# Hash-bucket attention and a maxout feed-forward on one core: query and key sets kept in load order, a second pair hashed by heads, the first batch dealt anew

## The chip, the core and the metric

The kernel runs on one core of one Trainium2 chip. The metric is the device time of one execution in microseconds (us); the kernel before took 266.97 us (median of three runs, 266.57 to 268.87). The core's engines are TensorE (PE; its weight loads are listed as PEld), VectorE (DVE), ScalarE (ACT), GpSimd (POOL) and SyncE (SP). ACT, POOL and SP also issue transfers. Each engine works through its own list of instructions in order; the lists are tied together by semaphores only.

## The reference

The inputs q, k and v have 4 batches, 8 heads, 768 tokens and 64 numbers per token and head, all fp32. Cut to what matters:

```
bits(x)  = (x @ proj) > 0                      # proj is 64 x 6: six bits per token and head
mask     = bucket(bits(q)) == bucket(bits(k))  # only tokens with the same six bits see each other
scores   = where(mask, q @ k.T / 8, -1e9)
attn     = softmax(scores) @ v
x        = attn, heads side by side: 3072 tokens x 512
h        = max(x @ w1, x @ w2, x @ w3)         # 512 -> 768
out      = h @ w_out                           # 768 -> 512
```

## The kernel before

**Scores.** For a head, a tile S holds the transposed queries or keys (64 rows, bf16) and below them the bits as +0.5 or -0.5, so that one matmul gives the scaled product plus a term that falls where bits differ. The work is cut into 192 units. A unit is two blocks of 128 keys against 384 queries (half the tokens) of one head: `scores(u)` (L274) issues two matmuls (L283) and ACT takes the exponential of both at once (L285) into one of 26 AT tiles. A batch is 48 units; a half batch of queries is 24, and its feed-forward can start when all eight heads of that half are done. The loop over units (L571) issues, for unit u: scores one or two units ahead, what `when(u, ...)` put down for u, one group of the feed-forward, the additions of AT tiles (`gather`, L327), and at the ends of stretches a `burst` (L542), which multiplies AT with the values (L310), sums AT over the keys (L360), inverts the sums and scales (L379) into the feed-forward's input xT. What is put down for a unit fixes only the place in each engine's list. SP's and POOL's transfers are issued as soon as their list has come to them and their buffer is free.

**First batch.** Its heads come in pairs 0 to 3, loaded in the order (p c): partition p holds tokens 6p to 6p+5. `load_pair` (L121) loads, `pair_group` (L145) transposes on PE (L132) and copies to a T32 tile on DVE or ACT (L138), `pair_place` (L140) scales on POOL into S (L143). Pair 0 is hashed head by head: `first_hash` (L171) puts each head's six rows of bits at the partitions where S wants them, and `first_bits` (L177) writes them from PSUM into S on DVE (L179). Pairs 1 to 3 go through `pair_hash` (L149): four matmuls (L154), one DVE comparison of 128 rows (L158) into a `bits` tile, and four transfers on SP from there into S (L163).

**Later batches.** Queries and keys come in sets of four heads, (side, g), side 1 the keys. `load_quad` (L184) loads a set in four transfers in the order (t cc m): partition t of a head's 32 holds, for each of four cc, six tokens m. `turn` (L193) transposes 32 x 32 blocks on DVE (L198), and writes them with a stride of four numbers, so that the columns stand in the order (m t cc), which is that of the values (`load_v`, L240, again p c). `narrow` (L200) scales to bf16 on POOL (L203), `place` (L207) moves to S by SP (L209), `quad_hash` (L212) hashes. Sets 2 and 3 belong to batch 1 and are dealt by hand inside the first batch; later ones follow a formula.

**Feed-forward.** `ffn_groups` (L385) gives, for half h (0 to 7), 18 groups of four matmuls (L394), six blocks of 128 hidden numbers by three weights, and six groups of the second product (L422). Of each block the first of three is copied from PSUM to ht as fp16 (L398, on ACT for even blocks and DVE for odd ones, on ACT at the end), and the next two are taken into ht as maxima by DVE (L400). The output rows of a block are set by `block_of`. From unit 39 one group is issued per unit.

**PSUM.** Score tiles rotate over s0 to s2 and all others over m0 to m3; s2 lies on m2 and m3 and is opened when unit MORE is issued (`lay_out`, L78).

Of the kernel before, what the change touches and what calls it, by code (L numbers as in the profile page):

```python
# [17 lines left out]
def kernel(  # L18
# [12 lines left out]
    nc = tc.nc  # L31
# [139 lines left out]
    def first_hash(bp, side, hd):  # L171
        for par in range(2):
            j = 2 * side + par
            nc.tensor.matmul(bp[Q * j : Q * j + NBITS, 0:HALF], pj2[:, par : 2 * NBITS : 2],
                             t32[0][:, side, hd * HALF : (hd + 1) * HALF], start=True, stop=True)

    def first_bits(bp, side, hd, par):  # L177
        j = 2 * side + par
        nc.vector.tensor_scalar(out=s_of[0][D : D + NBITS, 2 * side + hd, par * HALF : (par + 1) * HALF],  # L179
                                in0=bp[Q * j : Q * j + NBITS, 0:HALF], scalar1=0.0, scalar2=0.5,  # L180
                                op0=AluOp.is_gt, op1=AluOp.subtract)
# [11 lines left out]
    def turn(name, u, half):  # L193
        if name not in t32:
            t32[name] = t32_pool.tile([P, 2, S], FP32, tag="T32", name="T32")
        i_ = nat[name].rearrange("p (cc m u d) -> p u m cc d", cc=CC, u=2, d=Q)[:, u, half * MH : (half + 1) * MH]
        o = t32[name][:, u, half * HALF : (half + 1) * HALF].rearrange("p (m t cc) -> p m cc t", t=Q, cc=CC)
        nc.vector.transpose(o, i_)  # L198
# [40 lines left out]

    def load_v(g):  # L240
        b, h0 = divmod(4 * g, H)
        nc.gpsimd.dma_start(v_tile(g)[:], v[b, h0 : h0 + 4].rearrange("h (p c) d -> p h (c d)", p=P))
# [84 lines left out]
    def gather(u):  # L327
        g, hd, kp = unit_of(u)
        if u < 48 or kp == 0:
            return  # L330
        if kp == 1:
            as_of[g, hd] = as_pool.tile([P, 2, HALF], FP16, tag="as", name="As")
        t, new = as_of[g, hd], at_tiles[u % NAT][:, :, 0:HALF]
        old = at_tiles[(u - 1) % NAT][:, :, 0:HALF] if kp == 1 else t[:]
        nc.vector.tensor_tensor(out=t[:], in0=old, in1=new, op=AluOp.add)  # L335
        if kp == 2 and u >= 144:
            nc.vector.tensor_tensor(out=t[:, 0, :], in0=t[:, 0, :], in1=t[:, 1, :], op=AluOp.add)
# [47 lines left out]
    def ffn_groups(h):  # L385
        b, qh = divmod(h, 2)
        xt = xts.pop(h)
        hts, gs = {}, []
        for fb in range(NFB):
            for wi in range(3):  # L390
                def go(fb=fb, wi=wi):
                    ps = ps_tile("l1")
                    for jc in range(NJC):
                        nc.tensor.matmul(ps[:, 0:HALF], w_sb[wi][:, jc, fb * P : (fb + 1) * P], xt[:, jc, :],  # L394
                                         start=(jc == 0), stop=(jc == NJC - 1))
                    if wi == 0:
                        hts[fb] = h_pool.tile([P, HALF], FP16, tag="ht", name="ht")
                        (nc.vector.tensor_copy if fb % 2 and not ended else nc.scalar.copy)(hts[fb][:], ps[:, 0:HALF])  # L398
                    else:
                        nc.vector.tensor_tensor(out=hts[fb][:], in0=hts[fb][:], in1=ps[:, 0:HALF], op=AluOp.max)  # L400
                gs.append(go)
# [35 lines left out]
    with tc.manual_schedule():  # L437
# [9 lines left out]
        load_pair(3, nc.sync)  # L447
        load_quad(1, 2, range(4), nc.sync)
# [12 lines left out]
        load_v(0)  # L461
# [8 lines left out]
        pair_keep(0, 0, 0, mq, nc.scalar.copy)  # L470
# [40 lines left out]
        for u, side, g, eng in ((8, 0, 2, nc.sync), (25, 1, 3, nc.sync), (27, 0, 3, nc.sync)):  # L511
            when(u, load_quad, side, g, range(4), eng)
        hash_at = {}
        for g in range(2, NPAIR // 2):
# [16 lines left out]
            hash_at[{2: 33, 3: 48}.get(g, UPB * b2 - 24 + 24 * i2)] = g  # L531
# [3 lines left out]
        ffn_at = {39: 0, 57: 1, **{24 * (h + 1) + 9: h for h in range(2, 2 * B - 1)}}  # L535
# [101 lines left out]
```

## Time and profile before

| | |
|---|---|
| median of three runs | 266.97 us |
| profiled execution, its own time | 268.83 us |
| its span, first to last instruction | 267.0 us |
| mean granted TensorE clock | 0.987 |
| exponentials on ACT | 192, 153.0 us |
| weights, values, queries and keys read from HBM | 25.17 MB |

A profile page gives busy time of each engine; the span in 40 slices; the chain of work that ended last; and groups of instructions by line, engine, operation and tile, with the mean time of one and the idle time before them. The windows view gives busy time in chosen stretches and the granted clock. The timeline lists instructions in order of time. A wait is put down to what came last by the profile.

### The profile page before, as it was taken

How to read it: one execution, taken by the hardware profiler on the slowest of the kernel's cores; microseconds unless marked ns; L12 is line 12 of the kernel's file. 1: busy time of each engine (PE TensorE's matmuls, PEld its weight loads, DVE VectorE, ACT ScalarE, POOL GpSimd, SP SyncE). 2: the span in 40 equal slices, each digit the busy share in tenths (PEclk: the TensorE clock that was granted, in tenths of full speed). 3: DMA queues.
4: the chain of work that ended last, by engine and by line, in shares of the span. 5: the costliest groups of instructions: out<-in, count | busy, mean ns of one | idle time of the engine just before them, and what ended most of it. 6: DMA issues, size and time to landing. Idle time of an engine off the chain costs nothing. (4 is left out here: it accounts for less than half of the span.)

```text
span 267.0 us, 5948 instructions
## 1 busy us (share of the span) xinstructions
PE 256.7 (96%) x2247; PEld 141.0 (53%) x2247; DVE 207.9 (78%) x447; ACT 177.8 (67%) x256; POOL 63.8 (24%) x104
## 2 busy tenths in 40 slices
PE   7969979999999999999999999999999999999995
PEld 3535424555555554555555554555555555564552
DVE  2823897887989899889989899889848995886361
ACT  4977956683898179953898189954898289802322
POOL 3693642560151413440151312110000000000000
PEclk9997988999999999999999999999999999999999
DMA  6989999988055731973064821920030002000303
GB/s 210 341 170 234 158 273 205 218 167 200 6 153 144 178 77 39 189 216 105 1 159 139 185 68 39 196 61 18 0 119 2 2 0 87 33 1 2 118 0 118
DMA packets 21171, 30.96 MB, mean 116 GB/s; under 512 B 2696, under 2 KB 15896, under 8 KB 21144
## 3 DMA queue, kind: packets, MB, share of 16 engines
q0 software_dynamic: 7936, 12.59, 24.8%
q1 hardware_dynamic: 12920, 17.62, 20.7%
q8 instruction: 17, 0.28, 0.4%
q10 hardware_dynamic: 288, 0.39, 0.4%
q14 instruction: 10, 0.08, 0.1%
HBM read 25.17 MB, written 6.29 MB: 118 GB/s over the span
## 5 line engine op out<-in xcount | busy, mean ns | idle before, releaser
L285 ACT ACTIVATE AT<-sc 128x768 f16<-128x768 f32 x192 | 153.0, 817 | 58.1 <-PE sc L283 53.2
L394 PE MATMUL l<-xT,w_sb 128*128 128x384 f16 x568 | 112.3, 326 | 0.1
L283 PE MATMUL sc<-S 72*128 72x384 bf16 (+1 forms) x384 | 92.9, 330 | 5.1 <-POOL T L203 2.0
L394 PEld LDWEIGHTS <-w_sb 128*128 128x128 f16 x576 | 55.4, 97 | 39.4 <-DVE xT L379 1.2
L400 DVE TENSOR_TENSOR ht<-ht,l 128x384 f16<-128x384 f16 x95 | 51.7, 546 | 20.2 <-PE l L394 18.6
L283 PEld LDWEIGHTS <-S 72*128 72x128 bf16 (+1 forms) x384 | 36.1, 98 | 39.3 <-issue 11.3
L203 POOL TENSOR_SCALAR T<-T 128x768 bf16<-128x768 f32 x24 | 20.4, 851 | 100.6 <-DVE T L198 50.9
L198 DVE STREAM_TRANSPOSE T<-nat 128x384 f32<-128x384 f32 x48 | 40.3, 861 | 0.1
L422 PE MATMUL l<-wout_sb,ht 128*128 128x512 f16 x138 | 36.7, 379 | 0.3
L310 PE MATMUL av<-AT,vo 128*32 128x385 f16 x744 | 35.4, 335 | 0.0
L335 DVE TENSOR_TENSOR As<-As,AT 128x768 f16<-128x768 f16 x48 | 28.1, 586 | 3.3 <-ACT AT L285 1.8
L335 DVE TENSOR_TENSOR As<-AT,AT 128x768 f16<-128x768 f16 x48 | 29.1, 606 | 2.0 <-ACT AT L285 2.0
L310 PEld LDWEIGHTS <-vo 128*32 128x32 f16 x768 | 19.7, 98 | 15.8 <-issue 6.8
L398 ACT CAST ht<-l 128x384 f16<-128x384 f32 x28 | 13.4, 480 | 14.4 <-DVE ht L400 7.4
L379 DVE SCALAR_TENSOR_TENSOR xT<-av,sv,rb 128x384 f16<-128x384 f32 (+1 forms) x35 | 21.6, 617 | 1.2
L422 PEld LDWEIGHTS <-ht 128*128 128x128 f16 x138 | 13.3, 97 | 14.3 <-DVE ht L400 2.3
L426 ACT COPY osb<-l 128x512 f32<-128x512 f32 x23 | 13.4, 583 | 7.2 <-PE l L422 6.7
L143 POOL TENSOR_SCALAR S<-T 64x768 bf16<-64x768 f32 (+1 forms) x17 | 12.4, 730 | 6.8 <-ACT T L138 4.1
L319 DVE STREAM_TRANSPOSE ys<-sm 128x384 f32<-128x384 f32 x9 | 5.2, 582 | 8.4 <-PE sm L360 8.3
L398 DVE CAST ht<-l 128x384 f16<-128x384 f32 x19 | 10.4, 550 | 0.4 <-PE l L394 0.4
L138 DVE COPY T<-mp 128x384 f32<-128x384 f32 x9 | 4.6, 553 | 6.2 <-PE mp L132 5.4
L367 DVE STREAM_TRANSPOSE rb<-rr 128x384 f32<-128x384 f32 x16 | 9.1, 569 | 0.1
(55 smaller groups left out, 121.3 us busy)
## 6 DMA issues: line engine op xcount, KB each, us to landing
out_dram<-osb SPq DMA_DIRECT2D x23, 256.0 KB
S<-T SPq DMA_DIRECT2D x48, 96.0 KB
vo<-in_v_dram POOLq DMA_DIRECT2D x8, 384.0 KB, 7.8
nat<-in_k_dram POOLq DMA_DIRECT2D x16, 192.0 KB, 4.0
nat<-in_q_dram POOLq DMA_DIRECT2D x16, 192.0 KB, 5.3
w_sb<-in_moe_w_dram POOLq DMA_DIRECT2D x6, 384.0 KB, 6.4
nat<-in_k_dram SPq DMA_DIRECT2D x10, 192.0 KB
nat<-in_q_dram SPq DMA_DIRECT2D x8, 192.0 KB
```

Of the source, the lines that this page charges most:

```text
L198: nc.vector.transpose(o, i_)
L203: nc.gpsimd.tensor_scalar(out=t16[name][:, u, :], in0=t32[name][:, u, :], scalar1=RS, scalar2=1.0, op0=AluOp.mult, op1=AluOp.mult)
L283: nc.tensor.matmul(sc[:, j, 0:HALF], s_of[kn][0 : D + nb, kx, m * P : (m + 1) * P], s_of[qn][0 : D + nb, qx, qh * HALF : (qh + 1) * HALF], ...
L285: nc.scalar.activation(at_tiles[u % NAT][:, :, 0:HALF], sc[:, :, 0:HALF], ActFn.Exp, bias=-SCALE * 0.25 * nb, scale=SCALE)
L310: nc.tensor.matmul(av[r * Q : (r + 1) * Q, 0 : HALF + 1], vt[:, x, c + w : c + D : D // Q], at_of(g, m, hd)[:, 0 : HALF + 1], start=(m == ...
L335: nc.vector.tensor_tensor(out=t[:], in0=old, in1=new, op=AluOp.add)
L379: nc.vector.scalar_tensor_tensor(out=o, in0=av[p0:p1, 0:HALF], scalar=sv[p0:p1, :], in1=rc[p0:p1, :], op0=AluOp.add, op1=AluOp.mult)
L394: nc.tensor.matmul(ps[:, 0:HALF], w_sb[wi][:, jc, fb * P : (fb + 1) * P], xt[:, jc, :], start=(jc == 0), stop=(jc == NJC - 1))
L398: (nc.vector.tensor_copy if fb % 2 and not ended else nc.scalar.copy)(hts[fb][:], ps[:, 0:HALF])
L400: nc.vector.tensor_tensor(out=hts[fb][:], in0=hts[fb][:], in1=ps[:, 0:HALF], op=AluOp.max)
L422: nc.tensor.matmul(ps[:, 0:DM], hts[fb][:, tb * P : (tb + 1) * P], wout_sb[:, fb, :], start=(fb == 0), stop=(fb == NFB - 1))
L426: nc.scalar.copy(osb[:], ps[:, 0:DM])
```

## The change

- `turn` writes its blocks without a stride. The columns of a set then stand in load order (m cc t). `load_v` loads the values of batches 1 to 3 in the same order, by four transfers of 32 partitions where one did it; batch 0 keeps its order and its one transfer.
- In batches 1 to 3 the feed-forward's input has its tokens in load order too. The copy and the two maxima of each block read PSUM in the order (m t cc), with a step of 32 fp32 numbers between neighbours, and write ht without a stride; from there all is as it was.
- Pair 1 is hashed by heads like pair 0, with `first_hash` and `first_bits`, its bits written by DVE into S. Pairs 2 and 3 still go through `pair_hash`.
- The first batch's work is put at other units: pair groups and hashes, the loads of pair 3, of sets 2 and 3, of weights and values, the turns of sets 2 and 3, the early sums and value products, the first feed-forward groups (unit 40 for 39). Set 3 is loaded by POOL for SP. One copy of pair 0 goes from ACT to DVE. `gather` begins at unit 36 for 48. MORE is 11 for 10.

```diff
-    def first_hash(bp, side, hd):
+    def first_hash(bp, side, hd, pi=0):
...
-                             t32[0][:, side, hd * HALF : (hd + 1) * HALF], start=True, stop=True)
+                             t32[pi][:, side, hd * HALF : (hd + 1) * HALF], start=True, stop=True)
...
-        o = t32[name][:, u, half * HALF : (half + 1) * HALF].rearrange("p (m t cc) -> p m cc t", t=Q, cc=CC)
-        nc.vector.transpose(o, i_)
+        nc.vector.transpose(t32[name][:, u, half * HALF : (half + 1) * HALF], i_)
...
     def load_v(g):
         b, h0 = divmod(4 * g, H)
-        nc.gpsimd.dma_start(v_tile(g)[:], v[b, h0 : h0 + 4].rearrange("h (p c) d -> p h (c d)", p=P))
+        t, src = v_tile(g), v[b, h0 : h0 + 4]
+        if b == 0:
+            nc.gpsimd.dma_start(t[:], src.rearrange("h (p c) d -> p h (c d)", p=P))
+            return
+        src = src.rearrange("h (t cc m) d -> cc t h (m d)", cc=CC, t=Q)
+        for cc in range(CC):
+            nc.gpsimd.dma_start(t[cc * Q : (cc + 1) * Q], src[cc])
...
-        if u < 48 or kp == 0:
+        if u < 36 or kp == 0:
             return
...
+        def as_l(ht):
+            return ht[:].rearrange("f (m t cc) -> f m t cc", cc=CC, t=Q) if b else ht[:]
...
+                    l = ps[:, 0:HALF]
+                    if b:
+                        l = l.rearrange("f (m cc t) -> f m t cc", cc=CC, t=Q)
                     if wi == 0:
                         hts[fb] = h_pool.tile([P, HALF], FP16, tag="ht", name="ht")
-                        (nc.vector.tensor_copy if fb % 2 and not ended else nc.scalar.copy)(hts[fb][:], ps[:, 0:HALF])
+                        (nc.vector.tensor_copy if fb % 2 and not ended else nc.scalar.copy)(as_l(hts[fb]), l)
                     else:
-                        nc.vector.tensor_tensor(out=hts[fb][:], in0=hts[fb][:], in1=ps[:, 0:HALF], op=AluOp.max)
+                        nc.vector.tensor_tensor(out=as_l(hts[fb]), in0=as_l(hts[fb]), in1=l, op=AluOp.max)
...
         load_pair(2, nc.sync)
-        load_pair(3, nc.sync)
-        load_quad(1, 2, range(4), nc.sync)
...
-        load_v(0)
...
-        pair_keep(0, 0, 0, mq, nc.scalar.copy)
+        pair_keep(0, 0, 0, mq, nc.vector.tensor_copy)
...
-        when(3, lambda: first_bits(rest[0], 0, 1, 1))
-
-        for pi, us, uh, cs in ((1, [2, 3, 3, 4], 5, [1, 0, 0, 0]), (2, [4, 5, 8, 8], 11, [0, 1, 0, 0]), (3, [12, 14, 15, 16], 20, [0, 1, 1, 0])):
+        when(2, lambda: first_bits(rest[0], 0, 1, 1))
+
+        def head_hash(pi, hd, last):
+            bp = parts[pi, hd] = ps_tile("bp")
+            for side in (1, 0):
+                first_hash(bp, side, hd, pi)
+            if last:
+                t32.pop(pi)
+
+        def head_bits(pi, hd, n):
+            side, par = ((1, 0), (0, 0), (1, 1), (0, 1))[n]
+            first_bits(parts[pi, hd], side, hd, par, pi)
+
+        parts = {}
+        for pi, us, hs, offs, by_head, cs in ((1, (1, 2, 2, 3), (3, 6), (0, 0, 0, 0), 0, (1, 1, 0, 1)),):
+            for u, c, (side, hd) in zip(us, cs, ((1, 0), (0, 0), (1, 1), (0, 1))):
+                when(u, pair_group, pi, side, hd, nc.scalar.copy if c else nc.vector.tensor_copy)
+                if hd == 1 or by_head:
+                    for par in range(2):
+                        when(u, pair_place, pi, side, par, *((hd, hd + 1) if by_head else ()))
+            for hd in range(2):
+                when(hs[hd], head_hash, pi, hd, hd == 1)
+                for n in range(4):
+                    when(hs[hd] + offs[n], head_bits, pi, hd, n)
+
+        for pi, us, uh, cs in ((2, [4, 6, 9, 9], 12, [0, 1, 0, 0]), (3, [10, 13, 13, 16], 19, [0, 0, 0, 0]),):
...
-        when(18, load_v, 1)
-        for n, u in enumerate([1, 7, 13, 14, 15, 17, 27, 32]):
+        when(12, load_v, 1)
+        for n, u in enumerate([2, 2, 12, 14, 16, 16, 28, 35]):
             when(u, load_weights, n // 2, n % 2)
-        for u, side, g, eng in ((8, 0, 2, nc.sync), (25, 1, 3, nc.sync), (27, 0, 3, nc.sync)):
+        when(5, load_pair, 3, nc.sync)
+        when(1, load_v, 0)
+        for u, side, g, eng in ((1, 1, 2, nc.sync), (11, 0, 2, nc.sync), (22, 1, 3, nc.gpsimd), (28, 0, 3, nc.gpsimd)):
             when(u, load_quad, side, g, range(4), eng)
...
-                    t0, dt = {2: (20, 22), 3: (35, 42)}[g][n], {2: 2, 3: 1}[g]
+                    t0, dt = {2: (19, 18), 3: (33, 41)}[g][n], {2: 2, 3: 1}[g]
...
-            hash_at[{2: 33, 3: 48}.get(g, UPB * b2 - 24 + 24 * i2)] = g
+            hash_at[{2: 32, 3: 48}.get(g, UPB * b2 - 24 + 24 * i2)] = g
...
-        ffn_at = {39: 0, 57: 1, **{24 * (h + 1) + 9: h for h in range(2, 2 * B - 1)}}
+        ffn_at = {40: 0, 56: 1, **{24 * (h + 1) + 9: h for h in range(2, 2 * B - 1)}}
...
-        quad_at((0, 1), *[14, 18, 23])
-        quad_at((2, 3), *[26, 29, 30])
-        firsts.setdefault(33, []).append(lambda: hash_due(33))
-
-        issued, MORE, LAST = 0, 10, 3 * UPB // 4
+        quad_at((0, 1), *[16, 19, 22])
+        quad_at((2, 3), *[25, 29, 32])
+        firsts.setdefault(32, []).append(lambda: hash_due(32))
+
+        issued, MORE, LAST = 0, 11, 3 * UPB // 4
...
-                    lay_out(sc=['s2', 's1', 's0'], ms=['m0', 'm1'])
+                    lay_out(sc=['s2', 's0', 's1'], ms=['m0', 'm1'])
```

More of the change, by code (lines that the diff above doesn't have):

```diff
@@ L174, in first_hash, with first_bits @@
             nc.tensor.matmul(bp[Q * j : Q * j + NBITS, 0:HALF], pj2[:, par : 2 * NBITS : 2],
-                             t32[0][:, side, hd * HALF : (hd + 1) * HALF], start=True, stop=True)
-    def first_bits(bp, side, hd, par):
+                             t32[pi][:, side, hd * HALF : (hd + 1) * HALF], start=True, stop=True)
+    def first_bits(bp, side, hd, par, pi=0):
         j = 2 * side + par
-        nc.vector.tensor_scalar(out=s_of[0][D : D + NBITS, 2 * side + hd, par * HALF : (par + 1) * HALF],
+        nc.vector.tensor_scalar(out=s_of[pi][D : D + NBITS, 2 * side + hd, par * HALF : (par + 1) * HALF],
                                 in0=bp[Q * j : Q * j + NBITS, 0:HALF], scalar1=0.0, scalar2=0.5,
```

## Prediction

> **What bounds the kernel now.** I read the page first, then the windows, then the chain that ended last, and then the timeline where PE stands still.
>
> ```profile
> span 267.0 us, 5948 instructions
> PE 256.7 (96%) x2247; PEld 141.0 (53%) x2247; DVE 207.9 (78%) x447; ACT 177.8 (67%) x256; POOL 63.8 (24%) x104
> ```
>
> PE is busy for 96%, but the share is a mean over two very different stages, which the windows show (columns: stretch, its length, then the busy time of PE, PEld, DVE, ACT, POOL, the granted clock, the DMA share, GB/s).
>
> ```profile
> 8.00:50.00 42.00, 36.98 (x383) 18.24 (x382) 28.40 (x56) 31.18 (x44) 21.92 (x31) 0.92 1.01 228
> 14.10:17.50 3.40, 2.77 (x19) 1.64 (x17) 1.04 (x3) 3.04 (x5) 3.15 (x4) 1.00 1.04 233
> 17.50:20.90 3.40, 1.73 (x15) 0.60 (x15) 0.45 (x2) 2.16 (x4) 2.86 (x5) 1.00 0.63 94
> 20.90:24.30 3.40, 3.40 (x20) 2.14 (x22) 1.09 (x2) 2.80 (x5) 0.00 (x0) 0.51 1.06 298
> 34.60:38.00 3.40, 1.42 (x21) 0.71 (x24) 3.33 (x6) 1.68 (x4) 1.98 (x3) 1.00 1.15 276
> 38.00:41.40 3.40, 3.40 (x42) 1.14 (x34) 3.12 (x7) 1.61 (x3) 2.25 (x4) 0.51 1.04 258
> 57.00:87.00 30.00, 29.87 (x238) 16.63 (x237) 25.89 (x49) 22.94 (x33) 8.85 (x14) 1.00 0.53 125
> 87.00:117.00 30.00, 29.93 (x269) 16.72 (x267) 27.32 (x55) 21.48 (x31) 9.63 (x15) 1.00 0.56 135
> 117.00:147.00 30.00, 29.93 (x269) 16.80 (x267) 27.31 (x54) 21.52 (x31) 7.97 (x14) 1.00 0.40 110
> ```
>
> From about 50 us on PE has no idle time worth the name: 0.27 us in 90. A unit there is four feed-forward and two score matmuls, 0.65 + 0.33 = 0.98 us in the chain:
>
> ```profile
> 167.71 0.65 PE l L394 x4
> 168.36 0.33 PE sc L283 x2
> ...
> 207.88 0.38 PE sm L360 x8
> ```
>
> DVE, at 27.3 of 30, is close behind but does not decide. So in this stage faster DVE work is worth almost nothing, and slower DVE work can cost. The first 50 us are the other stage: no feed-forward is available, ACT works 31.18 of 42 us, PE stands still in places, and two stretches of 3.4 us run at a clock of 0.51, each right behind a stretch in which PE did little (1.73 and 1.42 of 3.40). What can be gained lies here. PE's two long waits:
>
> ```profile
> 14.57 3.27 SPq L163 DMA_DIRECT2D S<-bits  x4
> ...
> 19.19 0.81 PE L283 MATMUL sc<-S 70*128 70x384 bf16 x4 [1.67 <-POOL S L143]
> ...
> 30.59 3.02 SPq L163 DMA_DIRECT2D S<-bits  x4
> ...
> 36.70 0.81 PE L283 MATMUL sc<-S 70*128 70x384 bf16 x4 [1.98 <-POOL T L203]
> ```
>
> Both stand behind bits that SP sends into S: pair 1's from 14.57 us, pair 3's from 30.59. For the second the DMA view of 30.6 to 35.2 us shows why: beside 1 packet each of two instruction queues, only POOL's software queue moved anything, though SP had issued all four.
>
> ```profile
> q0 software_dynamic: 533, 0.91, 110.1%
> ...
> S<-bits SPq DMA_DIRECT2D x4, 9.0 KB
> ```
>
> The names given as releasers (POOL) are the work that happened to end last; S of pair 3 was placed long before.
>
> **The change part by part.** The groups that price it (busy us, mean ns of one):
>
> ```profile
> L400 DVE TENSOR_TENSOR ht<-ht,l 128x384 f16<-128x384 f16 x95 | 51.7, 546 | 20.2 <-PE l L394 18.6
> L198 DVE STREAM_TRANSPOSE T<-nat 128x384 f32<-128x384 f32 x48 | 40.3, 861 | 0.1
> L335 DVE TENSOR_TENSOR As<-AT,AT 128x768 f16<-128x768 f16 x48 | 29.1, 606 | 2.0 <-ACT AT L285 2.0
> L398 ACT CAST ht<-l 128x384 f16<-128x384 f32 x28 | 13.4, 480 | 14.4 <-DVE ht L400 7.4 <-PE l L394 7.1
> L367 DVE STREAM_TRANSPOSE rb<-rr 128x384 f32<-128x384 f32 x16 | 9.1, 569 | 0.1
> L191 POOL DMA_DIRECT2D nat<-in_k_dram x16 | 8.9, 561 | 0.3
> L242 POOL DMA_DIRECT2D vo<-in_v_dram x8 | 6.4, 801 | 0.1
> L337 DVE TENSOR_TENSOR As<-As 128x384 f16<-128x384 f16 x16 | 5.7, 358 | 0.5
> L179 DVE TENSOR_SCALAR S<-bp 6x384 bf16<-6x384 f32 x8 | 4.4, 555 | 1.8 <-PE bp L174 1.7
> L158 DVE TENSOR_SCALAR bits<-bp 128x384 bf16<-128x384 f32 x3 | 1.7, 558 | 3.5 <-PE bp L154 3.4
> ```
>
> *Turns.* Of the same size, the 48 strided transposes take 861 ns and those written without a stride 569. I take the stride to be the difference: 48 x 0.292 = 14.0 us of DVE. On the path it is worth 0, up to the 0.3 us that PE idles in those 90 us.
>
> *Maxima and copies.* Six half batches have 12 maxima each, and all but the last three copies each on DVE: 72 + 15 = 87 DVE operations (21 more copies on ACT) now read PSUM with a step of 128 bytes. No row shows a strided PSUM read. The nearest rows are a read with the same step from SBUF, and the strided write above:
>
> ```profile
> L320 DVE TENSOR_SCALAR rr<-ys x10: 172/182/690, 25.9 to 236.9; 128x24 f32<-128x24 f32 x6, 128x12 f32<-128x12 f32 x4
> ```
>
> With 12 numbers at a step of 32 the least is 172 ns, with 24 at a step of 16 the median is 182: 12 more strided reads cost 10 ns, 0.8 ns each, where a maximum has 546 / 384 = 1.4 ns per number to spend. By this row the extra x is 0; by the write row it is 0.29 us per operation; below 0 is excluded, since the step can only take runs apart. I take 0, because the change strides a read and not a write, and keep 0.29 as the slower rival. On ACT, 21 copies with x = 0.29 would be 6 us on an engine with 8 of 30 us free.
>
> *Values.* Six loads become 24: 18 more issues at 0.56 to 0.80 us, 10 to 14 us on POOL's list, spread over 150 us of an engine busy for 24%. They go out some 20 units ahead, against 7.8 us to landing on the page: 0.
>
> *Pair 1.* Four SP issues and the wait for their landing go. Eight comparisons of 0.555 for one of 0.558 put 3.9 us on DVE, which in 14.1 to 20.9 us works 1.5 of 6.8: hidden, if it does not come just ahead of a copy that PE waits for. PE's wait was 1.67; I take -1.4 (from -1.7 to 0, if POOL's placing is late next).
>
> *SP's and POOL's lists.* Without pair 1's bits in front of them, SP's loads of set 2 and pair 3 are issued one behind the other. POOL now places pair 0 ahead of the load of v (0.95 us earlier by that issue) and takes eight loads of set 3, 8 x 0.56 = 4.5 us, off SP; POOL's 21.92 of 42 us leaves room. Weights and v of units 13 to 18 are issued from 12 to 16, so that the software queue is emptier when pair 3's hash comes, a unit earlier (19 for 20). PE's 1.98 us at 36.70 should mostly go: -1.8, between -2.0 and 0. Next late would be POOL's set 3.
>
> *Clock.* If both waits go, PE has no empty stretch ahead of the two slow ones. Each slow stretch loses 3.4 x 0.49 = 1.7 us of PE work, 3.3 together. ACT shares the pace there, so I take half, -1.7 (from -3.3 to 0). The Trainium skill, "TensorE: Matmul & The Clock Gate", Part 1, says that the clock falls to half after an idle window of about 3.4 us, and that busy windows bring it back. The 0.51 stretches agree; by that rule the sum would take the whole 3.3.
>
> *Sums.* From unit 36 on AT is added up by DVE: 8 additions of 0.6, 4.8 us more, and at unit 48 PE has 8 sums where it had 24: 1.14 us (below) less 0.38 (above), -0.76.
>
> ```profile
> 45.93 1.14 PE L360 MATMUL sm<-AT,ones 128*32 128x384 f16 x24
> ...
> 49.70:57.00 7.30, 7.30 (x47) 4.32 (x46) 6.94 (x12) 6.62 (x11) 5.45 (x8) 1.00 0.73 192
> ```
>
> DVE is at 6.94 of 7.30 us just there; six of the additions (3.6 us) fall into units 40 to 47 and four shorter turns give 1.2 back. I charge +0.5 (0 to 2.4).
>
> *Feed-forward a unit later:* four matmuls fewer under one of the early units, +0.65 at most, +0.3 taken. Pair 0's copy on DVE, MORE and the order of the rings: 0, within 0.3 either way, as ACT loses 0.48 where DVE gains 0.55.
>
> Sum: -1.4 - 1.8 - 1.7 - 0.76 + 0.5 + 0.3 = -4.9 us. The profiled execution took 268.83 us, 1.8 around its span of 267.0, and would come to 264.0; the median of the runs lies 1.86 below it, at 266.97, and comes to **262.1**.
>
> **The rivals.**
>
> *Slower: the strided PSUM read costs what the strided write does.* Where turns run beside first-layer groups, DVE's list decides how much it may cost:
>
> ```profile
> 154.72 0.86 DVE L198 STREAM_TRANSPOSE T<-nat 128x384 f32<-128x384 f32 x1
> ...
> 157.28 0.87 DVE L198 STREAM_TRANSPOSE T<-nat 128x384 f32<-128x384 f32 x1
> 157.98 0.56 DVE L400 TENSOR_TENSOR ht<-ht,l 128x384 f16<-128x384 f16 x1
> 158.44 1.10 DVE L335 TENSOR_TENSOR As<-AT,AT 128x768 f16<-128x768 f16 x1
> ```
>
> A turn, two maxima and two additions took 2.56 us; half a copy adds 0.23, against three units of PE, 2.94. With the turn 0.29 shorter, 2.50 + 2.5x passes 2.94 at x = 0.18 us. At x = 0.29 each such triple is 0.3 too long, 0.55 where an addition takes 1.10 for 0.55 in every second one. Some 16 triples in halves 2 to 4 give 5 to 9 us; 10 more without turns (0.57 less, and 0.30 for L337) at 0.1 to 0.2 give 1 to 2. I take 8: 262.1 + 8 = **270.1**. It outweighs the gain from x of about 0.25 us on. For it speaks the 861; against it the 0.8 ns. The Trainium skill, "SBUF — State Buffer", Door 1, gives lines of 16 bytes in SBUF and 8 bytes in PSUM, with a penalty for each access that crosses to a new line; by that rule both strides here pay, the transposes' 861 agrees, and the time would be this rival's.
>
> *Level: the waits move instead of going.* POOL's queue is as full from 12 to 28 us as it was at 30.6 to 35.2, and holds pair 2's bits, or set 2's loads in front of DVE's turns at unit 18; then a slow clock stretch follows as before. Of the sum only -0.76 and one wait's share are left: **266**. For it speaks that SP's transfers moved nothing for 4.6 us; against it that pair 2's bits are due only some 10 units behind their hash.
>
> *The turns do not get shorter*, because the blocks' read pattern and not the write stride makes 861. With x = 0 PE still covers DVE's 27.3 of 30; only the crowd at unit 40 gets dearer, by 4 x 0.29 = 1.2 at most: **263**.
>
> **How the numbers follow.** The forecast has 0.54, the unshortened turns 0.07, the moved waits 0.19, the costly read 0.20. About 1% (2.7 us) is what a measurement of this kernel tells from no change. The first two lie below 264.3 nearly always, which makes faster 0.60; the moved waits and the fringe, same 0.20; the costly read, slower 0.20. With all terms at their good ends the forecast is 266.97 - 1.7 - 2.0 - 3.3 - 0.76 - 0.3 = 258.9, at the poor ends near 267. For 8 in 10 the range goes from 258 into the costly read, to 271; the forecast's own is 259 to 265.
>
> **What would show it.** Right: L198 near 570 ns; L400 near 546 and L398 as before; no wait of PE above 1 us between 14 and 38 us; fewer slices under full clock in the head; the first L394 some 5 us earlier than 49.77; PE still at 29.9 of 30 behind it. Wrong: L400 at 0.75 us or more, PE idle behind DVE's maxima between 80 and 145 us; or scores that again wait for a landing, with a slow stretch behind.

## The result, and the profile after

The changed kernel takes 264.47 us (median of 20 runs, 263.0 to 266.51), the kernel before 266.69 us beside it (20 runs, 265.01 to 270.73). The ratio is 0.9919, 95% interval [0.9893, 0.9945]: a gain of 0.8%, where 262.1 us and 1.8% were forecast. The direction is right, the size less than half.

The profiled execution of the changed kernel took 263.36 us, span 261.3. That is 5.5 less than the profiled execution of before, and close to the 264.0 to which the prediction's sum came for that execution. So the sum fits the two profiles and does not fit the two medians. The signs that the prediction named for being right hold in that profile too: turns at 564 ns, maxima at 548, no wait of PE above 0.63 us between 14 and 38 us, a full clock. The contradiction between profiles and medians is what the experiments are about.

The page after; its rows answer to those of the prediction (L197 was L198, L413 was L400, L411 was L398, L341 was L335, L248 was L242):

```profile
span 261.3 us, 5963 instructions
...
PE 253.6 (97%) x2239; PEld 140.4 (54%) x2239; DVE 206.0 (79%) x463; ACT 176.3 (67%) x255; POOL 79.3 (30%) x130
...
L413 DVE TENSOR_TENSOR ht<-ht,l 128x384 f16<-128x384 f16 x95 | 52.0, 548 | 18.0 <-PE l L404 16.5
...
L197 DVE STREAM_TRANSPOSE T<-nat 128x384 f32<-128x384 f32 x48 | 26.6, 564 | 0.1
L411 ACT CAST ht<-l 128x384 f16<-128x384 f32 x28 | 13.4, 479 | 10.4 <-DVE ht L413 7.4
...
L248 POOL DMA_DIRECT2D vo<-in_v_dram x24 | 13.3, 571 | 3.3 <-DMA wout_sb<-in_moe_w_out_dram 3.2
```

A turn takes 564 ns where it took 861; a maximum takes 548 where it took 546, though 72 of the 95 now read PSUM with a step of 128 bytes. DVE's total falls by 1.9 us only (206.0 for 207.9): by the groups, whose sums count overlapping ends twice, the turns lose 13.7 us, and the additions (62.3 for 57.2), the comparisons into S (8.9 for 4.4) and one more copy (0.7) take 10.3 of it back.

The windows after, with the prediction's columns:

```profile
8.00:50.00 42.00, 39.28 (x419) 20.01 (x418) 35.69 (x73) 35.60 (x52) 31.69 (x47) 1.00 1.02 224
14.10:17.50 3.40, 2.53 (x19) 0.99 (x18) 3.28 (x7) 2.99 (x6) 3.17 (x6) 1.00 1.19 283
17.50:20.90 3.40, 3.40 (x27) 1.97 (x26) 2.42 (x5) 3.40 (x6) 2.46 (x4) 1.00 1.02 203
20.90:24.30 3.40, 3.40 (x41) 2.18 (x37) 2.06 (x4) 3.06 (x6) 3.25 (x5) 1.00 0.45 47
34.60:38.00 3.40, 3.40 (x59) 1.67 (x55) 2.93 (x8) 3.25 (x5) 3.26 (x5) 1.00 0.59 196
38.00:41.40 3.40, 3.40 (x54) 1.62 (x50) 3.30 (x7) 1.99 (x4) 2.88 (x6) 1.00 0.87 143
...
87.00:117.00 30.00, 30.00 (x282) 17.04 (x278) 25.67 (x54) 21.18 (x30) 10.54 (x16) 1.00 0.55 145
```

Where before had PE at 1.73 and 1.42 of 3.40 us, each with a stretch at a clock of 0.51 behind it, there is now a full PE and a full clock. DVE falls from 27.32 to 25.67 of 30 us in the late stage. The timeline of the head (the first 50 us) has two rows in which PE's scores wait for a landing, both short, and SP's list has no transfer of pair 1's bits, only the eight of pairs 2 and 3:

```profile
21.91 8.51 SPq L163 DMA_DIRECT2D S<-bits  x8
...
28.77 0.48 PE L289 MATMUL sc<-S 70*128 70x384 bf16 x2 [0.29 <-DMA S<-bits]
...
33.69 0.81 PE L289 MATMUL sc<-S 70*128 70x384 bf16 x4 [0.40 <-DMA S<-bits]
...
45.73 0.81 PE L404 MATMUL l<-xT,w_sb 128*128 128x384 f16 x4
```

The first feed-forward group starts at 45.73 us, 4.0 earlier than 49.77.

To place the differences, the table cuts the span at the starts of the exponentials of some units, as the trace has them (us). It runs ahead to the experiments: "again" is another execution of an unchanged kernel, and the last two columns are the kernels of experiments 9 and 11.

| from ... to | before | before, again | after | after, again | group at 40 | weights later |
|---|---|---|---|---|---|---|
| start to unit 0 | 8.05 | 8.86 | 8.28 | 8.70 | 8.75 | 8.35 |
| unit 0 to 12 | 11.66 | 10.30 | 11.12 | 11.12 | 10.40 | 11.09 |
| unit 12 to 40 | 30.32 | 27.26 | 25.88 | 25.93 | 27.87 | 25.96 |
| unit 40 to 49 | 8.76 | 8.75 | 8.78 | 10.08 | 8.48 | 8.48 |
| unit 49 to 50 (burst) | 5.43 | 5.44 | 4.78 | 4.79 | 5.43 | 4.78 |
| unit 50 to 191 | 168.33 | 168.32 | 167.23 | 167.21 | 167.23 | 167.22 |
| unit 191 to end | 34.46 | 34.47 | 35.26 | 35.27 | 35.02 | 35.28 |
| span | 267.0 | 263.4 | 261.3 | 263.1 | 263.2 | 261.2 |
| mean granted clock | 0.987 | 0.999 | 0.999 | 0.999 | 0.999 | 1.0 |

The second profile of before is 3.6 us shorter than the first, all of it in the first 40 units.

### The profile page after: what moved, and what is told of

Same layout as the page of the kernel before. It is cut to its first block, busy times and chain, and to the rows that moved or that the text cites. A ratio compares the mean times of both kernels' runs of the same rounds, so it can differ in the third digit from the quotient of the medians.

```text
span 261.3 us, 5963 instructions
## 1 busy us (share of the span) xinstructions
PE 253.6 (97%) x2239; PEld 140.4 (54%) x2239; DVE 206.0 (79%) x463; ACT 176.3 (67%) x255; POOL 79.3 (30%) x130
## 4 chain that ended last, share of the span: by engine, by line
PE 84%; DVE 6%; DMA 6%; issue 1%; POOL 1%; ACT 1%; SPq 0%; DVEq 0%
PE l L404 34%; PE sc L289 20%; PE l L435 11%; PE av L316 9%; DMA nat<-in_q_dram 4%; PE bp L218 2%; DMA S<-bits 2%; PE sm L366 2%; PE mp L132 2%; DVE S L179 1%; PE bp L174 1%; PE wp L476 1%; DVE T L197 1%; DVE xT L385 1%; DVE ys L325 1%
## 5 line engine op out<-in xcount | busy, mean ns | idle before, releaser
L289 PE MATMUL sc<-S 72*128 72x384 bf16 (+1 forms) x384 | 91.4, 326 | 2.5 <-ACT AT L291 1.7
L413 DVE TENSOR_TENSOR ht<-ht,l 128x384 f16<-128x384 f16 x95 | 52.0, 548 | 18.0 <-PE l L404 16.5
L202 POOL TENSOR_SCALAR T<-T 128x768 bf16<-128x768 f32 x24 | 22.8, 948 | 76.1 <-DVE T L197 49.1
L435 PE MATMUL l<-wout_sb,ht 128*128 128x512 f16 x138 | 36.0, 378 | 0.0
L341 DVE TENSOR_TENSOR As<-AT,AT 128x768 f16<-128x768 f16 x52 | 29.0, 558 | 8.3 <-ACT AT L291 8.3
L341 DVE TENSOR_TENSOR As<-As,AT 128x768 f16<-128x768 f16 x52 | 33.3, 640 | 2.7 <-ACT AT L291 0.5
L316 PE MATMUL av<-AT,vo 128*32 128x385 f16 x744 | 34.2, 327 | 0.0
L197 DVE STREAM_TRANSPOSE T<-nat 128x384 f32<-128x384 f32 x48 | 26.6, 564 | 0.1
L411 ACT CAST ht<-l 128x384 f16<-128x384 f32 x28 | 13.4, 479 | 10.4 <-DVE ht L413 7.4
L248 POOL DMA_DIRECT2D vo<-in_v_dram x24 | 13.3, 571 | 3.3 <-DMA wout_sb<-in_moe_w_out_dram 3.2
L191 POOL DMA_DIRECT2D nat<-in_k_dram x20 | 11.1, 566 | 1.4 <-DMA vo<-in_v_dram 1.1
L191 POOL DMA_DIRECT2D nat<-in_q_dram x20 | 11.1, 567 | 1.1 <-DMA nat<-in_k_dram 0.8
L179 DVE TENSOR_SCALAR S<-bp 6x384 bf16<-6x384 f32 x16 | 8.9, 554 | 2.3 <-PE bp L174 2.0
```

The lines of the kernel that those rows point to most:

```text
L191: eng.dma_start(nat[side, g][:, cc * w : (cc + 1) * w], src[cc])
L197: nc.vector.transpose(t32[name][:, u, half * HALF : (half + 1) * HALF], i_)
L202: nc.gpsimd.tensor_scalar(out=t16[name][:, u, :], in0=t32[name][:, u, :], scalar1=RS, scalar2=1.0, op0=AluOp.mult, op1=AluOp.mult)
L289: nc.tensor.matmul(sc[:, j, 0:HALF], s_of[kn][0 : D + nb, kx, m * P : (m + 1) * P], s_of[qn][0 : D + nb, qx, qh * HALF : (qh + 1) * HALF], ...
L316: nc.tensor.matmul(av[r * Q : (r + 1) * Q, 0 : HALF + 1], vt[:, x, c + w : c + D : D // Q], at_of(g, m, hd)[:, 0 : HALF + 1], start=(m == ...
L413: nc.vector.tensor_tensor(out=as_l(hts[fb]), in0=as_l(hts[fb]), in1=l, op=AluOp.max)
```

## The experiments

**1. The kernel before, unchanged, profiled again.** One theory was that the profiled execution behind the prediction was a poor one and that its long waits and slow stretches are not in most executions; the rival, that they are in all of them and the change moved its waits elsewhere.

> The kernel before, unchanged, for a second profile and for the clocks and spans of its executions. Theory A (lucky and unlucky executions): the profiled execution of before (268.83 us, clock 0.987, two stretches of 3.4 us at half clock, each worth 0.0064 of the mean clock) was a bad one; most executions show a mean clock of 0.993 to 1.0 and spans from 263 to 266, and the second profile shows none or one such stretch. Theory B (the median execution of before is like the profiled one, and after loses something in most of its executions that its profile does not show): nearly all executions of before show 0.987. Both: ratio 1.000 within 0.003.

Measured: 268.42 us (265.19 to 270.4, 12 runs), ratio 1.0026 [0.9979, 1.0074]; profiled execution 265.25, span 263.4. Its windows and the one long wait left in its scores:

```profile
17.50:20.90 3.40, 3.28 (x26) 1.67 (x25) 1.58 (x3) 3.40 (x6) 3.16 (x6) 1.00 0.40 35
20.90:24.30 3.40, 3.40 (x42) 2.12 (x41) 1.85 (x4) 3.23 (x6) 1.41 (x3) 1.00 1.07 231
34.60:38.00 3.40, 3.40 (x56) 1.52 (x55) 3.26 (x8) 2.33 (x3) 2.16 (x3) 1.00 1.08 333
38.00:41.40 3.40, 3.00 (x29) 1.02 (x31) 3.13 (x7) 2.46 (x4) 1.88 (x3) 1.00 1.13 273
```

```profile
34.20 0.81 PE L283 MATMUL sc<-S 70*128 70x384 bf16 x4 [1.32 <-DMA S<-bits]
```

No wait at 19 us, 1.32 us in front of unit 30, no slow stretch. The mean granted clock of 88 executions of before is on record. One stretch of 3.4 us at half the clock takes 3.4 x 0.49 / 263 = 0.0063 off the mean, and the clocks of before fall into four groups at about that distance:

| slow stretches (mean clock) | executions of before | median us |
|---|---|---|
| none (0.998 to 1.0) | 20 | 265.30 |
| one (0.992 to 0.994) | 37 | 266.96 |
| two (0.986 to 0.987) | 18 | 268.75 |
| three (0.979 to 0.981) | 13 | 270.40 |

A slow stretch costs 1.6 to 1.8 us. The median execution of the 88 has one; the one profiled had two. The shares vary: of the 18 executions that ran beside experiments 5 to 8, 10 had two or three. The first theory holds for the slow stretches. The waits vary too. In the profiles of experiments 3 and 9, whose first batch is dealt as in before, PE waits 0.61 and 0.40 us in front of unit 12 (1.67 and none in the two profiles of before), and 2.40 and 2.65 in front of unit 30 (1.98 and 1.32).

**2. PE kept busy in front of the two waits.** Eight products of zeros go ahead of the scores of units 12 and 30, into the score tile that these then overwrite; no score changes.

```diff
+        if u in (12, 30):
+            for n in range(8):
+                nc.tensor.matmul(sc[:, n % 2, 0:HALF], warm[:, 0:P], warm[:, :], start=True, stop=True)
```

> The kernel before with 8 matmuls of zeros ahead of the scores of units 12 and 30, written to the score tile that the real scores then overwrite; they run while PE waits for the bits of pairs 1 and 3, so PE is not idle there, and nothing else changes. If slow clock stretches follow from PE's idleness, they go. Theory A: the median has about one such stretch or less to lose, so 0 to 1.5 us faster (ratio 0.994 to 1.000). Theory B: 2 to 3.3 us faster (0.988 to 0.993). If the clock stays slow, idleness in those two places does not set it.

Measured: 266.42 us (12 runs), ratio 0.9990 [0.9958, 1.0022]. The profiled execution took 683 us (unit 50 to 191 took 454 us where it takes 168) and is left aside, for a reason that is not known; the other eleven are all at the full clock, median 266.41. Before has 20 of 88 there. The trace of experiment 10, which has the same fillers, shows what they leave of the two waits, 0.58 and 1.20 us:

```profile
17.95 1.47 PE L288 MATMUL sc<-warm 128*128 128x384 f16 x8
20.00 0.81 PE L291 MATMUL sc<-S 70*128 70x384 bf16 x4 [0.58 <-DMA S<-bits]
...
33.82 1.47 PE L288 MATMUL sc<-warm 128*128 128x384 f16 x8
36.48 0.81 PE L291 MATMUL sc<-S 70*128 70x384 bf16 x4 [1.20 <-DMA S<-bits]
```

So no slow stretch comes where PE's gaps in these two places are partly filled. The fillers cost 266.41 - 265.30 = 1.1 us themselves, which uses up the gain.

**3. Load order alone.** The kernel before with the unstrided turns, the values in four transfers and the reads in (m t cc).

```diff
-        o = t32[name][:, u, half * HALF : (half + 1) * HALF].rearrange("p (m t cc) -> p m cc t", t=Q, cc=CC)
-        nc.vector.transpose(o, i_)
+        nc.vector.transpose(t32[name][:, u, half * HALF : (half + 1) * HALF], i_)
...
+                    if b:
+                        l = l.rearrange("f (m cc t) -> f m t cc", cc=CC, t=Q)
```

> The kernel before with the load order of the later sets alone: transposes without a stride, the values of batches 1 to 3 by four transfers, the strided PSUM reads of the copies and maxima. My sum: transposes 570 ns for 861, maxima 546 as before, the time unchanged (0 to -0.5 us, ratio 0.998 to 1.000), since PE is full where the sets' work lies. Rival: DVE's 14 us matter somewhere, 1 us or more faster (below 0.996).

Measured: 266.84 us (12 runs, one of which took 676 us, unexplained like the 683 above), ratio 0.9963 [0.9920, 1.0006], undecided; at the full clock 264.1, from 2 executions only. From unit 50 to 191 it takes 167.31 us instead of 168.32. The prediction put nothing there, because the windows gave PE 29.93 of 30. But the waits view of the kernel before (waiting engine and line, releaser, us in total, times, longest) has this row, the view of this run has none like it, and the timelines of DVE and PE in the kernel before show how it comes:

```profile
PEld L422 <- DVE ht L400: 2.3, 4, 0.6
```

```profile
101.18 0.86 DVE L198 STREAM_TRANSPOSE T<-nat 128x384 f32<-128x384 f32 x1
101.90 0.52 DVE L400 TENSOR_TENSOR ht<-ht,l 128x384 f16<-128x384 f16 x1
102.36 0.52 DVE L335 TENSOR_TENSOR As<-AT,AT 128x768 f16<-128x768 f16 x1
102.81 0.53 DVE L400 TENSOR_TENSOR ht<-ht,l 128x384 f16<-128x384 f16 x1
...
102.74 1.05 PE L422 MATMUL l<-wout_sb,ht 128*128 128x512 f16 x3
```

The second product of a half batch needs the last maximum. That stands behind a strided turn, another maximum and an addition and ends at 103.34; the three matmuls, 0.81 us elsewhere, take 1.05. It happens in four half batches, 0.22 to 0.29 us each by the starts of the matmuls: 1.0 in all. A matmul is listed with 326 ns and the next one starts after 162, so such a gap hides under a PE that looks busy. With the shorter turn it is gone.

**4. Pair 1's hash by heads alone,** in the deal of before, at units 4 and 5.

```diff
-            when(uh, pair_hash, pi)
+            if pi == 1:
+                when(4, head_hash, 1, 0)
+                when(5, head_hash, 1, 1)
+            else:
+                when(uh, pair_hash, pi)
```

> The kernel before with pair 1 hashed by heads and its bits written by DVE, at units 4 and 5; the places of all else as before. My sum: PE's wait of 1.67 us at 19 us goes, -1.4 us, and one slow clock stretch with it where there was one, up to -1.7 more: ratio 0.988 to 0.995. Rival: the wait passes to POOL's placing or the time is not on the path: 0.997 to 1.002.

Measured: 270.82 us (12 runs), ratio 1.0036 [0.9987, 1.0085], undecided by the interval; at equal clocks it is plainly slower: 267.13 at the full clock (4 executions, before 265.30), and 8 of 12 with two or three slow stretches. Timeline and windows of its profiled execution:

```profile
13.66 2.26 DVE L179 TENSOR_SCALAR S<-bp 6x384 bf16<-6x384 f32 x4 [0.45 <-PE bp L174]
...
16.54 2.26 DVE L179 TENSOR_SCALAR S<-bp 6x384 bf16<-6x384 f32 x4
18.83 0.56 DVE L138 COPY T<-mp 128x384 f32<-128x384 f32 x1
...
18.85 0.71 PE L132 MATMUL mp<-iden,nat 128*128 128x128 f32 x3 [0.76 <-DVE S L179]
```

```profile
17.50:20.90 3.40, 2.64 (x13) 1.51 (x12) 2.39 (x5) 2.16 (x4) 2.01 (x3) 0.74 0.99 288
20.90:24.30 3.40, 3.40 (x16) 1.29 (x15) 0.56 (x1) 2.14 (x4) 1.53 (x3) 0.50 0.72 124
24.30:27.70 3.40, 3.40 (x28) 1.74 (x29) 0.56 (x1) 2.11 (x4) 0.73 (x1) 0.50 0.43 84
```

Four comparisons stand on DVE as a block of 2.26 us. PE's next transposes wait 0.76 us for the last of them, and DVE's next copy comes only behind them. Here the clock is at half for more than two stretches.

**5 to 8. The kernel after, whole and with one part undone.** These four were measured beside each other, with the kernel before at 268.16 us (18 runs).

> The changed kernel, unchanged, for a second profile and the clocks of its executions. Theory A (the profiled execution of before was a bad one, with two slow clock stretches and a long hold-up of its transfers): ratio 0.992 again, clocks near 1.0. Theory B (after loses something in most executions that its profile does not show): the second profile shows a wait of 1 us or more in the first 50 us that the first has not. Both may hold in part: its own profiled execution lay 1.1 us below its median.

Measured: 264.46 us (7 runs), ratio 0.9901 [0.9864, 0.9939]; all seven at the full clock.

**6.** Pair 1 by `pair_hash` again:

```diff
-            for hd in range(2):
-                when(hs[hd], head_hash, pi, hd, hd == 1)
-                for n in range(4):
-                    when(hs[hd] + offs[n], head_bits, pi, hd, n)
+            when(4, pair_hash, pi)
```

> The changed kernel with pair 1 hashed by four matmuls, one comparison and four transfers again (at unit 4), all else as changed. My sum: pair 1's bits by DVE are worth 1.4 us and what the clock adds: 1.4 to 3 us slower than the changed kernel, ratio to before 0.997 to 1.003. Rival: with the first batch dealt anew the four transfers land in time, and the by-head hash is worth nothing (0.990 to 0.994).

Measured: 270.27 us (6 runs), ratio 1.0134 [1.0082, 1.0186]; two to four slow stretches in all six (mean clocks 0.973 to 0.987). So in the new deal the kernel without the hash by heads is 5.8 us slower than the kernel after; three stretches at 1.7 us each would be 5.1 of that, and no execution at the full clock shows what is left. In the old deal (experiment 4) the hash by heads costs 1.8 at the full clock and brings slow stretches. It has no price of its own.

**7.** The additions from unit 48 again:

```diff
-        if u < 36 or kp == 0:
+        if u < 48 or kp == 0:
```

> The changed kernel with the additions of AT tiles beginning at unit 48 again. My sum: PE has 0.76 us more of sums at unit 48, DVE 8 additions less; net between 0.26 us slower and 0.5 faster than the changed kernel: ratio 0.990 to 0.994. Rival: the DVE crowd between units 36 and 48 costs 1 us or more, and this runs faster than 0.989.

Measured: 264.09 us (6 runs), ratio 0.9896 [0.9853, 0.9940]: no different from the kernel after.

**8.** Strided turns, values and reads in the old order again (experiment 3's edit undone in the kernel after):

> The changed kernel with the strided transposes, the values' one load and the unstrided copies and maxima back, all else as changed. My sum: 14 us more on DVE, hidden behind PE except in the crowd between units 36 and 48, where eight transposes are 0.29 longer: 0 to 2 us slower than the changed kernel, ratio 0.991 to 0.999, and PE idle behind DVE there. Rival: nothing (0.990 to 0.993).

Measured: 266.49 us (12 runs), ratio 1.0001 [0.9963, 1.0039]; 266.36 at the full clock against 264.46: 1.9 us for the load order in the new deal. Its profile places it in the head: unit 12 to 40 takes 28.25 us where the kernel after takes 25.88 to 25.92. Two waits of PE make up 2.3 of these, the first 1.13 where the kernel after has 0.40, the second with no counterpart there:

```profile
34.50 0.81 PE L290 MATMUL sc<-S 70*128 70x384 bf16 x4 [1.13 <-DMA S<-bits]
...
40.17 1.50 PE L219 MATMUL bp<-T,pj 128*32 128x384 f32 x16 [1.58 <-DVE xT L386]
```

DVE's list there has eight turns ahead of this last matmul row, each some 0.3 us longer than in the kernel after. But from unit 50 to 191 it takes 167.22 us, although its turns are as long as before. So the shorter turn is enough to end PE's small wait there, and something in the new deal is enough as well. That led to the next run.

**9. The first feed-forward group at unit 40,** in the kernel before.

```diff
-        ffn_at = {39: 0, 57: 1, **{24 * (h + 1) + 9: h for h in range(2, 2 * B - 1)}}
+        ffn_at = {40: 0, 57: 1, **{24 * (h + 1) + 9: h for h in range(2, 2 * B - 1)}}
```

> The kernel before with one number changed: the first feed-forward group is dealt to unit 40 instead of 39. Since one group goes out per unit and the halves queue up behind each other, this puts every later group a unit later beside the turns and additions, which stay where they are. Theory that the place decides: the last maximum of a half batch no longer stands behind a turn and an addition on DVE, PE's wait of 0.23 us ahead of the second product goes in four or more half batches, and from the exponential of unit 50 to that of unit 191 it takes 167.2 to 167.4 us instead of 168.3; at the full clock the time is about 264.3 instead of 265.3. Rival, only the length of the turns decides: 168.3 stays, and a group put off costs up to 0.65: 265.3 to 266.0 at the full clock. As in the kernel before, slow stretches of the clock come and go between executions; times are compared at equal granted clock.

Measured: 265.38 us (12 runs), ratio 0.9960 [0.9926, 0.9995]; at the full clock 264.81 (6 executions) against 265.50 of the kernel before beside it. In the column "group at 40" of the table, unit 50 to 191 takes 167.23. Its waits view and DVE's list at the same place:

```profile
PEld L422 <- DVE ht L400: 0.2, 1, 0.2
```

```profile
98.83 0.54 DVE L400 TENSOR_TENSOR ht<-ht,l 128x384 f16<-128x384 f16 x1
99.29 0.55 DVE L335 TENSOR_TENSOR As<-As,AT 128x768 f16<-128x768 f16 x1
99.76 0.54 DVE L400 TENSOR_TENSOR ht<-ht,l 128x384 f16<-128x384 f16 x1
100.22 0.85 DVE L198 STREAM_TRANSPOSE T<-nat 128x384 f32<-128x384 f32 x1
```

One group goes out per unit and the halves queue up behind each other, so one number puts the groups of all halves a unit later, while turns and additions stay. The last maximum now comes ahead of the turn. The group put off appears at the end: unit 191 to the end takes 35.02 for 34.47. Unit 40 to 49 takes 8.48 for 8.75. These three, -1.1, +0.55 and -0.3, are about the full-clock gain of 0.7.

**10. Fillers and load order together:** the edits of experiments 2 and 3 in the kernel before.

> The kernel before with sets and values in load order, and with the eight zero matmuls ahead of the scores of units 12 and 30 that keep PE busy there (they change no score); the dealing, pair 1's hash and the sums are those of the kernel before. Theory that the gain of the whole change is an even clock plus the end of PE's 0.2 us waits plus the sums: the granted clock is 0.997 or more in nearly all executions, and the median 264.8 to 265.6, ratio about 0.992, with the sums' 0.66 and the better landings still missing. Rival, the parts do not add up: slow stretches come back, or the fillers cost time, and the median is 266.4 or more.

Measured: 265.28 us (264.57 to 266.1, 12 runs), ratio 0.9954 [0.9928, 0.9980]; all twelve at the full clock. Two edits that each gave an interval with 1 in it give a gain when taken together. At the full clock there is little of it (265.28 against 265.50): the load order's 1.0 us pays for the fillers' 1.1, and what is left is the slow stretch of the median execution.

**11 and 12. Set 3's queries ahead of the second weights.** In the kernel after, unit 40 to 49 takes 8.78 us in one profile and 10.08 in the other. The second one's timelines of POOL, DVE and PE:

```profile
39.66 1.68 POOL L248 DMA_DIRECT2D vo<-in_v_dram  x3
43.70 0.55 POOL L248 DMA_DIRECT2D vo<-in_v_dram  x1 [2.37 <-DMA wout_sb<-in_moe_w_out_dram]
45.96 0.75 POOL L254 DMA_DIRECT2D wout_sb<-in_moe_w_out_dram  x1 [1.71 <-DMA nat<-in_q_dram]
...
49.88 0.58 DVE L197 STREAM_TRANSPOSE T<-nat 128x384 f32<-128x384 f32 x1 [2.36 <-DMA nat<-in_q_dram]
...
50.95 0.81 PE L404 MATMUL l<-xT,w_sb 128*128 128x384 f16 x4 [0.68 <-DVE ht L413]
```

POOL waits 2.37 and 1.71 us with an issue for earlier landings. This wait is the program's own: by the semaphores that the trace records with each instruction, POOL's transfers use eight semaphores in turn, and each first waits until the last transfer that used the same one, eight issues earlier, has landed. So a transfer on POOL's list needs more than a free buffer. The fourth load of values stands eight behind a load of w_out. In the kernel after the values take four of these eight places where one load took one, and in experiment 8, with one load of values, neither wait appears. DVE waits 2.36 us for set 3's queries, then has turns, additions and maxima all at once, and PE waits for a maximum. The edit deals the two loads of w_out, of which one was issued in front of these queries, to units 36 and 40:

```diff
-        for n, u in enumerate([2, 2, 12, 14, 16, 16, 28, 35]):
+        for n, u in enumerate([2, 2, 12, 14, 16, 16, 36, 40]):
```

> The kernel after, with the two loads of the second weight matrix dealt to units 36 and 40 instead of 28 and 35, so that set 3's queries stand ahead of both on POOL's list. Theory that set 3's late queries cost the kernel after up to 1.3 us between units 40 and 49: DVE's wait for them (2.4 us at 48 to 50 us) goes, unit 40 to unit 49 takes 8.5 to 8.8 us in every execution, and the median is 263.4 to 264.1 where the kernel after has 264.4. Rival, the transfers only change places (values late, or weights late at unit 58): 264.4 or more.

Measured: 263.32 us (263.1 to 264.02, 6 runs), ratio 0.9883 [0.9853, 0.9913] to the kernel before, all at the full clock. Unit 40 to 49 takes 8.48 us, and DVE's turn of set 3's queries follows its addition without a wait:

```profile
47.14 0.55 DVE L341 TENSOR_TENSOR As<-AT,AT 128x768 f16<-128x768 f16 x1
47.61 0.56 DVE L197 STREAM_TRANSPOSE T<-nat 128x384 f32<-128x384 f32 x1
```

The same with the additions from unit 48:

> The same as the one before it in this call, and the additions begin at unit 48 again instead of 36. Theory that the eight additions pay once set 3 is no longer late: this is slower than the kernel with additions from unit 36 by 0.3 to 0.7 us (the burst at unit 49 takes 5.44 us instead of 4.78). Rival, DVE's crowd between units 40 and 48 is the cost: this is faster by 0.2 to 0.5 us.

Measured: 264.31 us (6 runs), ratio 0.9911 [0.9878, 0.9944], 1.0 slower than with the additions from unit 36. So the eight additions pay only once set 3 is in time; experiment 7, with set 3 late, could not see it. The kernel of experiment 11 is the fastest of all: 1.2% below the kernel before, and its 263.32 stand against 264.46 and 264.47 of the kernel after, which was not measured beside it.

## Why the direction was right and the size was not

**The step that failed first: carrying the sum over to the median.** The prediction made its sum on one execution and then wrote that "the median of the runs lies 1.86 below it, at 266.97, and comes to 262.1". That takes the difference between the execution and the median for a constant. It was itself one slow stretch more (two against one, 268.75 - 266.96 = 1.8). The change takes away what made that execution poor, so the 1.86 was counted twice: in the terms and in the offset. Of the kernel after, 24 of 27 executions have no slow stretch; the 17 of these among the 20 of the result have a median of 264.28.

**"I take -1.4" and "-1.8" for the two waits.** Together -3.2; mis-sized. At the full clock, unit 0 to 40 goes from 10.30 + 27.26 = 37.56 to 11.12 + 25.88 = 37.00: -0.56. From the profiles of experiments 3 and 9, with the same deal at the full clock (38.19 and 38.27), it would be -1.2 and -1.3, still less than half. The wait for pair 1's bits, 1.67 in the profile that was priced, is 0 to 0.61 in the other three. The one for pair 3's is there (1.32 to 2.65) and falls to 0.40; units 12 to 40 gain 1.4 against before again. But the first twelve units lose 0.8 in the new deal, the same in both profiles of the kernel after. By ACT's timelines there, ACT waits for PE 0.62 us in one and 0.75 in the other, and makes four copies of pairs' tiles between its exponentials where it made two, at some 0.36 us each: that accounts for the 0.8. So most of pair 1's wait, like the second slow stretch, belonged to the execution that was profiled. Against that execution all that was predicted does come: 41.98 to 37.00, -5.0 where the terms were -1.4 - 1.8 - 1.7.

**Clock, -1.7.** Against the median this is right in size by luck: not "half of 3.3", but the whole of one slow stretch, 1.66 us, goes from the median execution. A stretch costs its whole 3.4 x 0.49, so halving it because ACT shares the pace was wrong. Experiments 2 and 10 show that PE's idleness in these two places brings it: of the 23 executions with fillers at ordinary times, none has one. The Trainium skill, "TensorE: Matmul & The Clock Gate", Part 1, has the half clock after an idle window of about 3.4 us. That is not enough to tell here when it comes: PE worked 1.42 us of the 3.40 ahead of a slow stretch in the first profile, and in experiment 9 it waited 2.65 us in front of unit 30 with no slow stretch behind. In the traces the clock changes only after whole multiples of 3.41 us. Counted in these steps, PE worked 1.78 and 1.43 us ahead of the slow ones of the first profile, and 1.99 and 2.19 in the two steps over which experiment 9's wait falls. But experiment 3's profile has a step of 1.76 with no slow one behind it, and experiment 4's one of 2.02 with three behind, so PE's busy time in a step does not decide alone.

**Sums, -0.76.** Right: the burst takes 4.78 for 5.44, -0.66; experiment 7 shows that in the kernel after the crowd at unit 40 takes it back.

**"Feed-forward a unit later", +0.3.** Wrong in sign. The late group is paid at the end (34.47 to 35.26, +0.79), but the shift ends PE's small waits from unit 50 to 191 (-1.09): -0.3 in sum. By experiments 3, 8 and 9 either the shorter turns or the shift would do, so the prediction's "worth 0" for the turns there holds in the new deal only by accident.

**Turns in the head.** A term put at nothing: outside the crowd they were given no price, but the load order is worth 1.9 us in the new deal, and its profile places it in the head, where PE waits behind DVE (experiment 8).

**Crowd at unit 40, +0.5, and POOL's loads, 0.** The extra issues were not free, though not by their 0.56 us each: with four loads for one, the values fill half of the eight places behind which POOL's next issue must wait. "Next late would be POOL's set 3" is what happened. It costs 0.0 in one profile (8.78 for 8.75) and 1.3 in the other; experiment 11 removes it.

**Strided PSUM read, x = 0.** Right: 548 ns against 546 for the maxima, 479 against 480 for the copies on ACT. This rival is out. The Trainium skill, "SBUF — State Buffer", Door 1, gives PSUM lines of 8 bytes and says that patterns there that are not contiguous slow matmuls; for these reads by DVE and ACT no run here shows a penalty. "The turns do not get shorter" is out by 564 against 861, and "the waits move" by the two short waits and the clock in the windows after.

Sum of what was found at the full clock, profile against profile (before again to after): -0.58 start, -0.56 head, +0.03 crowd, -0.66 burst, -1.09 late stage, +0.79 end: -2.1 of span. The -0.58 at the start is no gain: the kernel after, profiled again, starts at 8.70. Medians at the full clock differ by 265.30 - 264.28 = 1.0, and the median execution of before has one slow stretch more, 1.7: 2.7. The result shows 266.69 - 264.47 = 2.2, because its 20 executions of before have a median 0.27 below the 266.96 of those with one slow stretch, and the three of the kernel after that have one lift its median by 0.19.

**What stays open.** Why one stall of PE is followed by a half clock and a longer one is not. What the hash by heads is worth at the full clock. That the two more copies on ACT cost the first twelve units their 0.8 us is read from timelines; no run undid them.

## What to carry to other kernels

Before pricing a wait seen in one profiled execution, compare that execution's granted clock and time with the other runs: a stall and the slow stretch behind it may belong to that execution alone, and their removal then cannot be subtracted from the median. A single number that sets a queue's first unit can shift everything queued behind it, so ask what each later item then stands behind on the other engines. Parts of such a deal do not add up; undo them one at a time in the new kernel, not only in the old.

## What the runs showed of the hardware

- The half clock comes in whole stretches of about 3.4 us, none to three in an execution of the kernel before, at 1.6 to 1.8 us each.
- DVE and ACT read PSUM with a step of 128 bytes as fast as without (548 and 546 ns, 479 and 480 ns for 128 x 384), while the strided write of a turn cost 861 for 564.
- Eight matmuls of zeros in front of two waits of PE left 0.58 and 1.20 us of the waits (experiment 10's trace) and no slow stretch in 23 executions, where 68 of 88 had one or more without them.
